# Scores over full 32-row tiles with zero rows, and PV with 32 weight columns

## The chip, the cores and the metric

The kernel runs on one core of a Trainium2 chip. The metric is the device time of one execution in microseconds (us). Before the change it is 1242.52 us, the median of three runs (1239.01 to 1251.18).

## The reference, cut to what matters

A layer norm of x (2048 rows of 512) feeds two branches, and both are added to x. Branch A is attention with 32 heads of 16 dimensions, branch B a gated feed-forward block with 1792 hidden columns.

```python
xn = _layernorm(x)
qkv = (xn @ wqkv)                                  # 2048 x 1536, 32 heads of 16
scores = jnp.einsum("bhqd,bhkd->bhqk", q, k) * (Dh ** -0.5)
p = _softmax(scores, axis=-1)
o = jnp.einsum("bhqk,bhkd->bhqd", p, v)
A = o @ wo
B = (_silu(xn @ w1) * (xn @ w3)) @ w2
return x + A + B
```

## The kernel before

Two programs are planned in Python and emitted, `_plan_fast` and `_plan_max`; the second is only entered when a flag says that the first was out of its numeric range, and it does not run here. All lines named below are of the fast one.

**How it is tiled.** Queries are cut into 4 chunks of 512, heads into 8 groups of 4. A unit is one chunk with one group, 32 units in all. In a unit the keys come in 16 tiles of 128. K and Q lie transposed in SBUF, in `KT` and `QT`: the four heads of a group stand on partitions 0, 32, 64 and 96, each with 16 rows of data and a 17th row of constants (1.0 in `QT`, 127 times 128 in `KT`). Partitions 17 to 31 of each 32 are never written and never read. The constants come from `crow`, four rows in the scratch tile `yb`, by two DMAs (L1095 and L1097).

**Scores** (`score`, L1509): one call issues two matmuls, of two heads, on two 32-row tiles of the array, with 17 rows of weights (`KT`, 128 keys) and 17 rows of moving data (`QT`, 512 queries), into two PSUM banks.

**Exponentials.** A pair of banks goes one of two ways. `try_a` gives it to ScalarE, one ACTIVATE of 128x1024 (L1543). `try_d` gives it to VectorE, which builds exp from integer operations (L1587, L1610, L1604, L1615, L1621) in three parts, and so makes three times as many PV matmuls. L1610 writes the scratch tile `mb`.

**PV** (`try_pv`, L1670): four matmuls side by side, one per head and per 32-column tile of the array. The weights are `Vaug[:, kt, head, :]`, 128 rows by 17 columns (16 of V and a column of ones, which gives the sum of the softmax), the moving data 128x512 probabilities. Results gather in PSUM bank 7, 17 of each 32 partitions; the other partitions of the bank hold zeros from the start. At the end of a unit L1687 copies the bank to `U`, four sums per query are turned into reciprocals by way of small DMAs, and L1723 multiplies `U` by `R`, whose unused partitions are zero.

**Dense matmuls** (`col_groups`, L1204): all projections, the feed-forward block and the output, always four matmuls side by side with 128 rows and 32 columns each.

**The order** is fixed at build time. A planner (`_Sched`) plays the engines' time with assumed costs, for TensorE 0.23 us per group of four, and writes one instruction list per engine. On TensorE it tries ScalarE scores first, then VectorE scores, PV and dense work. Work for the other engines waits in lists filled by `post` and emptied by `pump`, by priority. All DMAs are issued from the SyncE queue in the planned order: the loads of x and wqkv, the constants, then for every K and Q tile the moves from a staging tile `stg` to `KT` and `QT` (L1279), the late loads of the feed-forward weights and wo (L1186 to L1198), and later the small DMAs at the end of each unit.

Of the kernel before, what the change touches and what calls it, by code (L numbers as in the profile page):

```python
# [140 lines left out]
class _Sched(_Prog):  # L141
# [28 lines left out]

    def post(self, eng, emit, ready=0.0, prio=1, cond=None):

        self.seq += 1
        self.pend[eng].append((prio, self.seq, ready, cond, emit))

# [802 lines left out]
def _plan_fast(nc, ps, flag, A_x, A_wqkv, A_wo, B_w1, B_w3, B_w2, out):  # L978
    S, D = A_x.shape[1], A_x.shape[2]
    H = D // 16  # L980
# [30 lines left out]
    with ctx:  # L1011
# [4 lines left out]
        yb = sb("yb", [128, 2, 1024], I16)  # L1016
        mb = sb("mb", [128, 2, 1024], I16)
        crow = yb[0:4, 0, :].bitcast(BF16).rearrange("p (k n) -> p k n", n=512)
        xn_sb = sb("xn_sb", [128, 4, D], BF16)
# [54 lines left out]
        def c_misc(e):  # L1074
            e.memset(crow[:, 0, :], 1.0)
            e.memset(crow[:, 1, :], YB)
            e.memset(ones_t[:, :], 1.0)
            return e.memset(mhalf[:, :], -0.5)
# [5 lines left out]
        for gi in range(1, 4):  # L1084
            P.dma(lambda e, gi=gi: e.dma_start(x_sb[:, 4 * gi:4 * gi + 4, :], x_v[:, 4 * gi:4 * gi + 4, :]),
                  writes=[("x", t) for t in range(4 * gi, 4 * gi + 4)], kb=512)
            if gi == 1:
                P.dma(lambda e: e.dma_start(wv, wqkv_v[:, :, 2 * D:3 * D]), writes=[("wv",)], kb=512)

        P.op("dve", lambda e: e.memset(bank(7), 0.0), writes=[("ps", 7)], dur=0.6)  # L1090
        P.op("pool", c_misc, writes=[("ones_t",), ("mhalf",), ("crow",)], dur=0.8)
        P.op("pool", lambda e: e.affine_select(ident[:, :], ones_t[:, :], [[1, 128]], ALU.is_equal, 0.0,
# [5 lines left out]
                                    crow[:, 1, :].unsqueeze(1).broadcast_to([4, NG * NQC, 512])),  # L1098
              reads=[("crow",)], writes=[("KTc",)], kb=128)

        def fill(eng_dst, val):
# [390 lines left out]
        def score(b0, name, dur):  # L1492
            r0 = st["pos"]
            u, rr = divmod(r0, RPU)
            kt, j0 = divmod(rr, 4)
            g = u % NG
            if not have(("QTm", u), ("KTm", g, kt // 4)):
                return None
            rd = [("QT", u % 4), ("KT", g, kt // 4), ("QTc",), ("KTc",)]
            mms = []  # L1500
            for i in range(2):
                j = j0 + i
                rd += [("QTm", u, j), ("KTm", g, kt // 4, j)]
                mms.append((b0 + i, KT[32 * j:32 * j + 17, g, kt * 128:(kt + 1) * 128],
                            QT[32 * j:32 * j + 17, u % 4, :], 32 * j))

            def f(e, mms=tuple(mms)):
                for (b, l_, r_, rp) in mms:
                    ins = e.matmul(bank(b), l_, r_, start=True, stop=True, tile_position=(rp, 0))  # L1509
                return ins  # L1510
            o = P.op("pe", f, reads=rd, writes=[("ps", b0), ("ps", b0 + 1)], dur=pe_dur("S", dur), name="%s%d" % (name, r0))
            st["pos"] += 2
            return r0, u, j0, kt, o
# [44 lines left out]
        def try_d():  # L1558
# [24 lines left out]
            def p1():  # L1583
# [25 lines left out]
                def f_m():  # L1609
                    P.op("dve", lambda e: e.tensor_scalar(mb[:, ys, :], yb[:, ys, :], 0x7F, 0x3F00,  # L1610
                                                          ALU.bitwise_and, ALU.bitwise_or),
                         reads=[("yb", ys)], writes=[("mb", ys)], dur=0.35)

# [18 lines left out]

        pv_unit = [0]

        def try_pv():
# [22 lines left out]
            for j in sorted(pick):  # L1658
# [4 lines left out]
                stop = st["pos"] >= (u + 1) * RPU and npv[u][j] == NT + 2 * ndj[u][j]  # L1663
                mms.append((j, Vaug[:, tk[1], 4 * g + j, :], tk[2], start, stop))
                rd += [("V", tk[1]), tk[3]]
                rels.append(tk[4])

            def f(e, mms=tuple(mms)):
                for (j, v_, p_, s0, s1) in mms:
                    ins = e.matmul(bank(PV)[32 * j:32 * j + 17, :], v_, p_, start=s0, stop=s1, tile_position=(0, 32 * j))  # L1670
                return ins
# [244 lines left out]
```

## Time and profile before

| | |
|---|---|
| time, median of 3 runs | 1242.52 us (1239.01 to 1251.18) |
| time of the profiled execution | 1237.0 us |
| its span, first to last instruction | 1235.1 us |
| instructions | 21867 |
| mean granted TensorE clock in the span | 0.595 of full speed |
| HBM read, written | 22.81 MB, 2.10 MB |

A page of the profile gives, for one execution, the busy time of each engine: PE is TensorE's matmuls, PEld its weight loads (they overlap the matmuls), DVE is VectorE, ACT ScalarE, POOL GpSimd, SPq the queue from which SyncE issues DMAs. PEclk is the TensorE clock that was granted: 0.50 is 1.2 GHz and 1.00 is 2.4 GHz; a value between them is a stretch with some of each. Matmuls are pipelined, and a busy PE is not one at its peak.

### The profile page before, as it was taken

The numbers are of one execution on the slowest core, as the hardware profiler recorded it, in microseconds if no ns is written. First come the engines' busy times: TensorE is split into PE (matmuls) and PEld (weight loads), VectorE is DVE, ScalarE is ACT, GpSimd is POOL, SyncE is SP. The second block draws the span as 40 slices with busy tenths as digits, with TensorE's granted clock in tenths as the row PEclk, the third lists the DMA queues.
The fourth block names the chain that finished last, engine by engine and source line by source line (L and its number), as shares of the span: only waits on it lengthen the run. The fifth ranks groups of instructions, "written<-read, shape, count | busy, mean of one in ns | idle before, by whom it ended". The sixth has DMA issues, their size and how long they took to land.

```text
span 1235.1 us, 21867 instructions
## 1 busy us (share of the span) xinstructions
PE 1155.8 (94%) x9033; PEld 233.0 (19%) x9033; DVE 829.9 (67%) x1434; ACT 843.2 (68%) x874; POOL 53.5 (4%) x72
## 2 busy tenths in 40 slices
PE   4799999999999999999999999998999999989656
PEld 2222111111111221111111111122211111121123
DVE  5368776677766997766777655689876766657322
ACT  4578777677776997777777666689877776647210
POOL 3000000000000000000000000010000000010000
PEclk9666555555555995555555555579655555575588
DMA  4402122220211131122222110032222210032220
GB/s 133 102 19 33 18 31 23 24 39 12 32 16 12 21 25 27 22 23 27 31 23 23 5 19 10 13 32 28 24 34 23 27 19 9 15 36 27 32 51 30
DMA packets 90837, 35.49 MB, mean 29 GB/s; under 512 B 74456, under 2 KB 88680, under 8 KB 90728
## 3 DMA queue, kind: packets, MB, share of 16 engines
q1 hardware_dynamic: 90728, 34.00, 19.8%
q8 instruction: 73, 1.20, 0.4%
q14 instruction: 36, 0.29, 0.1%
HBM read 22.81 MB, written 2.10 MB: 20 GB/s over the span
## 4 chain that ended last, share of the span: by engine, by line
PE 84%; DVE 8%; DMA 4%; SPq 1%; issue 1%; ACT 1%; POOL 0%; DVEq 0%; POOLq 0%
PE ps L1509 29%; PE ps L1204 29%; PE ps L1670 26%; DVE f_yb L1587 3%; DMA f_w<-in_B_w_dram 2%; DMA f_KT<-f_stg 1%; DVE f_xd L1621 1%; DVE f_mb L1610 1%; DVE f_xd L1604 1%; DMA f_wkv<-in_A_wqkv_dram 1%; DVE f_xd L1615 1%; ACT f_PT L1543 1%; SPq L1279 0%; PE ps L1233 0%; DVE f_hT L1356 0%
## 5 line engine op out<-in xcount | busy, mean ns | idle before, releaser
L1543 ACT ACTIVATE f_PT<-ps 128x1024 bf16<-128x1024 f32 x798 | 798.8, 1027 | 298.8 <-PE ps L1509 258.7
L1509 PE MATMUL ps<-f_QT,f_KT 17*128 17x512 bf16 x2048 | 452.9, 563 | 17.8 <-DMA f_KT<-f_stg 7.4
L1587 DVE TENSOR_SCALAR f_yb<-ps 128x1024 int16<-128x1024 f32 x226 | 276.1, 1222 | 135.6 <-PE ps L1509 127.4
L1670 PE MATMUL ps<-f_PT,f_Vaug 128*17 128x512 bf16 x1596 | 331.7, 562 | 7.3 <-DVE f_xd L1604 5.3
L1670 PE MATMUL ps<-f_xd,f_Vaug 128*17 128x512 bf16 x1356 | 303.9, 570 | 2.9 <-DVE f_xd L1621 2.2
L1204 PE MATMUL ps<-f_xnT,f_w 128*32 128x512 bf16 x1792 | 230.7, 576 | 26.2 <-DMA f_w<-in_B_w_dram 23.7
L1509 PEld LDWEIGHTS ps<-f_QT,f_KT 17*128 17x128 bf16 x2048 | 84.7, 98 | 546.3 <-issue 341.4
L1621 DVE TENSOR_TENSOR f_xd<-f_yb,f_mb 128x1024 bf16<-128x1024 bf16 x226 | 152.3, 683 | 0.0
L1610 DVE TENSOR_SCALAR f_mb<-f_yb 128x1024 int16<-128x1024 int16 x226 | 101.1, 447 | 5.4
L1604 DVE TENSOR_SCALAR f_xd<-f_yb 128x1024 int16<-128x1024 int16 x226 | 100.4, 444 | 0.0
L1204 PE MATMUL ps<-f_w,f_hT 128*32 128x512 bf16 x896 | 97.8, 509 | 2.3 <-DVE f_hT L1356 1.3
L1615 DVE TENSOR_SCALAR f_xd<-f_yb 128x1024 int16<-128x1024 int16 x226 | 96.8, 428 | 0.1
L1356 DVE SCALAR_TENSOR_TENSOR f_hT<-f_t,ps 128x512 bf16<-128x512 bf16 x56 | 38.4, 686 | 74.1 <-PE ps L1204 73.8
L1723 POOL TENSOR_TENSOR f_onorm<-f_U,f_R 128x512 bf16<-128x512 f32 x31 | 41.6, 1342 | 1054.5 <-DMA f_R<-f_Rrow 560.6
L1670 PEld LDWEIGHTS ps<-f_PT,f_Vaug 128*17 128x17 bf16 x1596 | 54.3, 93 | 137.3 <-issue 101.2
L1204 PEld LDWEIGHTS ps<-f_xnT,f_w 128*32 128x32 bf16 x1792 | 47.8, 110 | 113.3 <-issue 76.7
L1670 PEld LDWEIGHTS ps<-f_xd,f_Vaug 128*17 128x17 bf16 x1356 | 49.7, 95 | 88.5 <-issue 53.1
L1342 ACT ACTIVATE f_th<-ps 128x512 f32<-128x512 f32 x56 | 33.6, 599 | 47.9 <-PE ps L1204 47.9
L1346 DVE SCALAR_TENSOR_TENSOR f_t<-f_th,ps 128x512 bf16<-128x512 f32 x56 | 38.2, 683 | 29.2 <-ACT f_th L1342 29.2
L1204 PE MATMUL ps<-f_wo,f_onorm 128*32 128x512 bf16 x512 | 53.0, 494 | 0.1
L1687 DVE COPY f_U<-ps 128x512 f32<-128x512 f32 x32 | 22.0, 689 | 33.4 <-PE ps L1670 28.4
L1204 PE MATMUL ps<-f_xnT,f_wq 128*32 128x512 bf16 x256 | 34.6, 575 | 0.3 <-DVE f_hT L1356 0.3
(48 smaller groups left out, 232.6 us busy)
## 6 DMA issues: line engine op xcount, KB each, us to landing
f_w<-in_B_w_dram SPq DMA_DIRECT2D x112, 128.0 KB, 2.5
f_R<-f_Rrow SPq DMA_DIRECT2D x128, 32.0 KB, 4.0
f_KT<-f_stg SPq DMA_DIRECT2D x128, 16.0 KB, 1.8
f_QT<-f_stg SPq DMA_DIRECT2D x128, 16.0 KB, 1.8
f_xr<-in_A_x_dram SPq DMA_DIRECT2D x16, 128.0 KB
out_dram<-f_xn_sb SPq DMA_DIRECT2D x16, 128.0 KB, 1.7
f_w<-in_B_w_dram SPq DMA_DIRECT2D x1, 1792.0 KB
f_xd<-in_A_x_dram SPq DMA_DIRECT2D x3, 512.0 KB
```

Source lines behind the costliest of these rows:

```text
L1204: ins = e.matmul(bank(bk)[32 * i:32 * i + 32, 0:ncols], make_lhsT(i), rhs_ap, start=start, stop=stop, tile_position=(0, 32 * i))
L1346: q2 = P.op("dve", lambda e: e.scalar_tensor_tensor(t1[:, ss, :], th[:, ss, :], 1.0, bank(bk), ALU.add, ALU.mult), reads=[("th", ss), ("ps ...
L1356: q = P.op("dve", lambda e: e.scalar_tensor_tensor(hT[:, fc, :], t1[:, ss, :], 0.5, bank(bk), ALU.mult, ALU.mult), reads=[("t1", ss), ("ps ...
L1509: ins = e.matmul(bank(b), l_, r_, start=True, stop=True, tile_position=(rp, 0))
L1543: q = P.op("act", lambda e: e.activation(PT[:, s_, :], ps[:, b0 * 512:(b0 + 2) * 512], ACTF.Exp, scale=ASC, bias=A_BIAS), reads=[("ps", b0 ...
L1587: q = P.op("dve", lambda e: e.tensor_scalar(yb[:, ys, :], ps[:, 4 * 512:6 * 512], 0.0, 32767.0, ALU.max, ALU.min), reads=[("ps", 4), ("ps" ...
L1604: q_ = P.op("dve", lambda e: e.tensor_scalar(dsl[:, s_, 0, :], yb[:, ys, :], 0x7F80, None, ALU.bitwise_and), reads=[("yb", ys)], writes=[( ...
L1610: P.op("dve", lambda e: e.tensor_scalar(mb[:, ys, :], yb[:, ys, :], 0x7F, 0x3F00, ALU.bitwise_and, ALU.bitwise_or), reads=[("yb", ys)], wr ...
L1615: q_ = P.op("dve", lambda e: e.tensor_scalar(dsl[:, s_, 1, :], yb[:, ys, :], -352.0, 0.0, ALU.add, ALU.max), reads=[("yb", ys)], writes=[( ...
L1621: q_ = P.op("dve", lambda e: e.tensor_tensor(dsl[:, s_, 2, :].bitcast(BF16), yb[:, ys, :].bitcast(BF16), mb[:, ys, :].bitcast(BF16), ALU.m ...
L1670: ins = e.matmul(bank(PV)[32 * j:32 * j + 17, :], v_, p_, start=s0, stop=s1, tile_position=(0, 32 * j))
L1723: q = P.op(eng, lambda e: e.tensor_tensor(onorm[:, u % NON, :], U[:, us, :], R[:, :], ALU.mult), reads=[("U", us)] + [("R", j_) for j_ in ...
```

## The change

Three things are edited.

- `KT` and `QT` get zeros on partitions 17 to 31 of every 32. The zeros come from `zrow`, 15 rows of the scratch tile `mb`, set by one more GpSimd memset and copied by 20 DMAs: four for `QT`, four for groups 0 and 1 of `KT` right after them, and twelve for the other six groups, posted to SyncE's list with the planner's time 14.0 us. The scores wait for them (keys `QTz` and `KTz`), and the first three writes of `mb` at L1610 wait until they have been read.
- The two matmuls of a score then take 32 rows in place of 17, zeros in the added ones.
- PV takes 32 weight columns of `Vaug` in place of 17, from the same start, so that the 15 added ones are the first columns of the next head. The last head keeps 17. What the added columns give lands on the partitions that nobody reads unscaled; `R` is zero there.

`post` gets a duration and a function `backlog` is added; neither is called with it here.

```diff
--- before.py
+++ after.py
@@ -168,10 +168,13 @@
         op = _Prog.dma(self, fn, reads, writes, name, eng)
         return self._time(op, op.deps, 0.06, 1.9 + kb / 200.0)
 
-    def post(self, eng, emit, ready=0.0, prio=1, cond=None):
+    def post(self, eng, emit, ready=0.0, prio=1, cond=None, dur=0.6):
 
         self.seq += 1
-        self.pend[eng].append((prio, self.seq, ready, cond, emit))
+        self.pend[eng].append((prio, self.seq, ready, cond, emit, dur))
+
+    def backlog(self, eng):
+        return max(0.0, self.free[eng] - self.t) + sum(it[5] for it in self.pend[eng] if it[2] <= self.t + 0.3)
 
     def pump(self, eng):
         best = None
@@ -1015,6 +1018,7 @@
         xr = sb("xr", [128, 2, D], BF16)
         yb = sb("yb", [128, 2, 1024], I16)
         mb = sb("mb", [128, 2, 1024], I16)
+        zrow = mb[0:15, 0, 0:512].bitcast(BF16)
         crow = yb[0:4, 0, :].bitcast(BF16).rearrange("p (k n) -> p k n", n=512)
         xn_sb = sb("xn_sb", [128, 4, D], BF16)
         stats = sb("stats", [128, NT, 6], FP32)
@@ -1074,6 +1078,7 @@
         def c_misc(e):
             e.memset(crow[:, 0, :], 1.0)
             e.memset(crow[:, 1, :], YB)
+            e.memset(zrow[:, :], 0.0)
             e.memset(ones_t[:, :], 1.0)
             return e.memset(mhalf[:, :], -0.5)
 
@@ -1088,7 +1093,7 @@
                 P.dma(lambda e: e.dma_start(wv, wqkv_v[:, :, 2 * D:3 * D]), writes=[("wv",)], kb=512)
 
         P.op("dve", lambda e: e.memset(bank(7), 0.0), writes=[("ps", 7)], dur=0.6)
-        P.op("pool", c_misc, writes=[("ones_t",), ("mhalf",), ("crow",)], dur=0.8)
+        P.op("pool", c_misc, writes=[("ones_t",), ("mhalf",), ("crow",), ("zrow",)], dur=0.8)
         P.op("pool", lambda e: e.affine_select(ident[:, :], ones_t[:, :], [[1, 128]], ALU.is_equal, 0.0,
                                                base=0, channel_multiplier=-1),
              reads=[("ones_t",)], writes=[("ident",)], dur=0.4)
@@ -1097,6 +1102,19 @@
         P.dma(lambda e: e.dma_start(KT[16:128:32, :, :].rearrange("p g (a n) -> p (g a) n", n=512),
                                     crow[:, 1, :].unsqueeze(1).broadcast_to([4, NG * NQC, 512])),
               reads=[("crow",)], writes=[("KTc",)], kb=128)
+
+        def zeros(g0, g1):
+            for j in range(4):
+                P.dma(lambda e, j=j: e.dma_start(
+                    KT[32 * j + 17:32 * j + 32, g0:g1, :].rearrange("p g (a n) -> p (g a) n", n=512),
+                    zrow[:, :].unsqueeze(1).broadcast_to([15, (g1 - g0) * NQC, 512])),
+                    reads=[("zrow",)], writes=[("KTz", g) for g in range(g0, g1)], kb=60 * (g1 - g0))
+        for j in range(4):
+            P.dma(lambda e, j=j: e.dma_start(QT[32 * j + 17:32 * j + 32, :, :],
+                                             zrow[:, :].unsqueeze(1).broadcast_to([15, 4, 512])),
+                  reads=[("zrow",)], writes=[("QTz",)], kb=60)
+        zeros(0, 2)
+        P.post("sp", lambda: [zeros(g, g + 2) for g in range(2, NG, 2)], ready=14.0, prio=2)
 
         def fill(eng_dst, val):
             return lambda e: e.activation(eng_dst, mhalf[:, 0:1].to_broadcast((128, eng_dst.free_size())), ACTF.Copy,
@@ -1500,9 +1518,9 @@
             mms = []
             for i in range(2):
                 j = j0 + i
-                rd += [("QTm", u, j), ("KTm", g, kt // 4, j)]
-                mms.append((b0 + i, KT[32 * j:32 * j + 17, g, kt * 128:(kt + 1) * 128],
-                            QT[32 * j:32 * j + 17, u % 4, :], 32 * j))
+                rd += [("QTm", u, j), ("KTm", g, kt // 4, j), ("QTz",), ("KTz", g)]
+                mms.append((b0 + i, KT[32 * j:32 * j + 32, g, kt * 128:(kt + 1) * 128],
+                            QT[32 * j:32 * j + 32, u % 4, :], 32 * j))
 
             def f(e, mms=tuple(mms)):
                 for (b, l_, r_, rp) in mms:
@@ -1609,7 +1627,7 @@
                 def f_m():
                     P.op("dve", lambda e: e.tensor_scalar(mb[:, ys, :], yb[:, ys, :], 0x7F, 0x3F00,
                                                           ALU.bitwise_and, ALU.bitwise_or),
-                         reads=[("yb", ys)], writes=[("mb", ys)], dur=0.35)
+                         reads=[("yb", ys)], writes=[("mb", ys)] + ([("zrow",)] if nd < ND else []), dur=0.35)
 
                 def f_g():
                     q_ = P.op("dve", lambda e: e.tensor_scalar(dsl[:, s_, 1, :], yb[:, ys, :], -352.0, 0.0,
@@ -1631,6 +1649,12 @@
             return True
 
         pv_unit = [0]
+        Vf = Vaug[:, :, :, :].rearrange("p t h d -> p t (h d)")
+
+        def v_w(kt, h):
+
+            return Vf[:, kt, 17 * h:17 * h + (32 if h < H - 1 else 17)]
+
 
         def try_pv():
             u = pv_unit[0]
@@ -1661,13 +1685,13 @@
                 start = npv[u][j] == 0
                 npv[u][j] += 1
                 stop = st["pos"] >= (u + 1) * RPU and npv[u][j] == NT + 2 * ndj[u][j]
-                mms.append((j, Vaug[:, tk[1], 4 * g + j, :], tk[2], start, stop))
+                mms.append((j, v_w(tk[1], 4 * g + j), tk[2], start, stop))
                 rd += [("V", tk[1]), tk[3]]
                 rels.append(tk[4])
 
             def f(e, mms=tuple(mms)):
                 for (j, v_, p_, s0, s1) in mms:
-                    ins = e.matmul(bank(PV)[32 * j:32 * j + 17, :], v_, p_, start=s0, stop=s1, tile_position=(0, 32 * j))
+                    ins = e.matmul(bank(PV)[32 * j:32 * j + v_.shape[-1], :], v_, p_, start=s0, stop=s1, tile_position=(0, 32 * j))
                 return ins
             o = P.op("pe", f, reads=rd, writes=[("ps", PV)], dur=pe_dur("C", 0.23), name="pv%d" % u)
             for r_ in rels:
```

## Rows read from the trace of the kernel before

**Rows 1.** Page, parts 1, 2, 4: busy us, granted clock by slices, chain

```profile
PE 1155.8 (94%) x9033; PEld 233.0 (19%) x9033; DVE 829.9 (67%) x1434; ACT 843.2 (68%) x874; POOL 53.5 (4%) x72
...
PEclk9666555555555995555555555579655555575588
...
PE 84%; DVE 8%; DMA 4%; SPq 1%; issue 1%; ACT 1%; POOL 0%; DVEq 0%; POOLq 0%
```

**Rows 2.** Windows: stretch, us, busy us (count) of each engine, PEclk, DMA share, GB/s

```profile
77.30:111.40 34.10, 34.10 (x238) 6.06 (x230) 26.58 (x45) 25.69 (x27) 1.40 (x1) 0.50 0.22 30
...
121.70:401.60 279.90, 278.46 (x1922) 48.49 (x1920) 195.84 (x333) 200.73 (x205) 10.56 (x8) 0.50 0.19 23
401.60:466.40 64.80, 60.21 (x692) 15.86 (x684) 62.04 (x108) 61.57 (x66) 4.19 (x3) 1.00 0.25 28
466.40:818.00 351.60, 350.76 (x2408) 59.52 (x2404) 242.70 (x418) 253.30 (x256) 11.71 (x9) 0.50 0.17 19
818.00:876.00 58.00, 51.62 (x548) 14.22 (x546) 56.03 (x97) 55.14 (x62) 4.74 (x4) 1.00 0.34 38
876.00:1084.20 208.20, 207.75 (x1438) 36.10 (x1442) 139.10 (x240) 145.91 (x149) 3.81 (x3) 0.50 0.14 19
...
1098.00:1150.00 52.00, 50.14 (x342) 8.82 (x346) 39.01 (x67) 36.82 (x39) 3.91 (x3) 0.50 0.24 29
```

**Rows 3.** Windows of L1543, the ScalarE exponentials

```profile
121.70:401.60 279.90, 194.46 (x193) 0.50 0.19 23
401.60:466.40 64.80, 61.08 (x65) 1.00 0.25 28
466.40:818.00 351.60, 246.76 (x243) 0.50 0.17 19
818.00:876.00 58.00, 53.47 (x57) 1.00 0.34 38
```

**Rows 4.** Windows of L1587, the first step of the VectorE exponentials

```profile
121.70:401.60 279.90, 67.16 (x55) 0.50 0.19 23
401.60:466.40 64.80, 24.43 (x20) 1.00 0.25 28
466.40:818.00 351.60, 88.03 (x72) 0.50 0.17 19
818.00:876.00 58.00, 19.53 (x16) 1.00 0.34 38
```

**Rows 5.** Windows of L1509, the scores: PE, PEld, PEclk, DMA share, GB/s

```profile
814.70:818.00 3.30, 0.27 (x4) 0.10 (x2) 0.50 0.49 55
...
108.00:111.40 3.40, 1.12 (x8) 0.21 (x6) 0.50 0.30 68
...
230.90:234.30 3.40, 1.18 (x6) 0.17 (x6) 0.50 0.08 20
```

**Rows 6.** Windows of L1670, PV, in the first stretch of rows 5

```profile
814.70:818.00 3.30, 3.15 (x28) 0.82 (x28) 0.50 0.49 55
```

**Rows 7.** Windows, all engines, the last 3.4 us before two falls of the clock

```profile
463.00:466.40 3.40, 2.17 (x28) 0.52 (x25) 3.26 (x5) 3.35 (x4) 1.27 (x1) 1.00 0.51 123
872.60:876.00 3.40, 2.36 (x22) 0.69 (x22) 3.29 (x7) 2.27 (x3) 0.00 (x0) 1.00 0.17 38
```

**Rows 8.** Groups by line: xcount | busy us, mean ns | idle before

```profile
L1670 PEld LDWEIGHTS ps<-f_PT,f_Vaug 128*17 128x17 bf16 x1596 | 54.3, 93 | 137.3 <-issue 101.2 <-DVE f_yb L1587 9.2 <-DVE f_xd L1604 9.1
...
L1204 PEld LDWEIGHTS ps<-f_xnT,f_w 128*32 128x32 bf16 x1792 | 47.8, 110 | 113.3 <-issue 76.7 <-DMA f_w<-in_B_w_dram 30.0 <-DVE f_hT L1356 1.1
```

**Rows 9.** SyncE's queue and chain of waits at the start: start us, us, what

```profile
8.43 0.56 SPq L1097 DMA_DIRECT2D f_KT<-f_yb  x1
19.20 5.03 SPq L1279 DMA_DIRECT2D f_KT<-f_stg  x8
...
34.13 11.15 DMA f_KT<-f_stg
```

**Rows 10.** Page, part 6: DMA issues, KB each, median us to landing

```profile
f_w<-in_B_w_dram SPq DMA_DIRECT2D x112, 128.0 KB, 2.5
```

## The prediction

> **What bounds the kernel now.** I read the page's first two parts first. TensorE is busy 94% of the span, VectorE 67%, ScalarE 68%, and the granted clock stands at 5 in 28 of the 40 slices [rows 1]; in the chain that ended last TensorE has 84% [rows 1]. So TensorE is the bound, at half its clock. Next the windows, cut where the clock changes [rows 2]. There are two kinds of stretch. At 0.50 TensorE is busy throughout (278.46 of 279.90 us, 350.76 of 351.60) while ScalarE and VectorE stand at 70%. At 1.00 TensorE has gaps (60.21 of 64.80) and ScalarE and VectorE are both at 95% (61.57 and 62.04 of 64.80): there they are the bound. The order of instructions is the same fixed list in both; only the clock differs.
>
> What a stretch gets done is counted in score pairs, of which every pair ends in one L1543 or one L1587. At half clock 193 + 55 and 243 + 72 pairs, 563 in 631.5 us, or 1.122 us each; at full clock 65 + 20 and 57 + 16, 158 in 122.8 us, or 0.777 us each [rows 3, 4]. Full clock is worth 1 - 0.777 / 1.122 = 31% of a half-clock stretch, not 50%, since the other two engines then set the pace.
>
> **What moves the clock.** Busy time does not: the two long half-clock stretches are busy over 99%. What the engine did ahead of a change differs. The clock rose at 818.0 us after 3.15 us of PV and 0.27 us of scores [rows 5, 6], and at 111.4 after 3.4 us with 1.12 us of scores; with 1.18 us of scores it did not rise at 234.3 [rows 5]. It fell at 466.4 and 876.0 after TensorE had been busy only 2.17 and 2.36 us of 3.4, waiting for the other two engines [rows 7]. Two things follow. PV with 17 of 32 columns lifted the clock by itself, so idle columns do not count against it. The scores hold it down: a pair of them drives 2 x 17 = 34 of the array's 128 rows, PV and dense work all 128. And the steady mix is near to rising as it is, since two stretches as alike as 1.12 and 1.18 us of scores came out differently.
>
> **Part 1, scores with 32 rows.** The pair then drives 64 of 128 rows. A matmul streams 512 columns as before, so its own time stays. If rows are what counts, a mix that is near to rising with 34 rows rises in most places with 64, and the clock comes up on its own rather than after a chance run of PV or dense work. Half-clock stretches in the middle: 34.1 + 279.9 + 351.6 + 208.2 + 52.0 = 925.8 us [rows 2]. At full clock they save 31%, or 285 us.
>
> The clock will still fall where TensorE waits, as in rows 7. The full-clock stretches of 64.8 and 58.0 us [rows 2] give one fall per 61 us; 925.8 - 285 = 641 us hold 10 or 11. No row shows how soon it comes back with 32 rows. The bounds are 0 and the 34.1 us that the shortest half-clock stretch of rows 2 lasted. I take 11 us, a third, because the mix as a rule rises then. Each costs 31% of that: 10.5 x 11 x 0.31 = 36 us, between 0 and 111.
>
> The Trainium skill speaks against this part. TensorE: Matmul & The Clock Gate, Part 1, says that the gate sets the clock by how busy the PE has been recently, and its section Why this matters for your kernels asks only for continuous busy time; by that the rows of a matmul would not matter, the kernel would already run at full clock, and the change would give the start-up cost only, about 1248 us. This trace does not agree, with 99% busy at 0.50 in rows 2.
>
> **Part 2, PV with 32 columns.** The load of 128x17 weights takes 93 ns, that of 128x32 takes 110 [rows 8]. For 2952 loads (1596 in the row shown, 1356 of the second PV source) that is 2952 x 17 ns = 50 us of loading. It lies beside matmuls: loads take 48.49 of 279.90 us and dense groups already load 32 columns [rows 2, 8]. Cost 0; 50 us if none of it were covered. Gain 0, as 17 columns lifted the clock in rows 6; a gain on top would only make the first part surer.
>
> **Part 3, the zeros.** One memset on GpSimd, busy 53.5 us in the whole span [rows 1], and 20 DMAs on SyncE's queue. A move of its kind occupies the queue 5.03 / 8 = 0.63 us [rows 9], so 20 are 12.6 us. The queue is free from 8.99 to 19.20 us [rows 9]; the eight that the first scores need, 5.0 us, fit in it, and stand ahead of the K and Q moves. The other twelve, 7.6 us, have 5.2 us of it if they come next, and otherwise stand ahead of the late loads and of the second K moves, whose landing TensorE already awaits for 11.15 us [rows 9]. So between 2.4 and 7.6 us are late on the queue. The copies also move 2.2 MB in pieces of some 120 KB; the nearest row is a 128 KB load that lands in 2.5 us [rows 10], 0 if all of it falls in the free time, up to 6 us if it pushes the late loads. I take 6 us on the path, between 0 and 14. The wait at L1610 costs nothing as long as the copies land before VectorE's first exponentials, and otherwise no more than the lateness already counted. What stands behind a late K move on SyncE's queue is the next K move, and for those wait scores and then ScalarE; later in the kernel nothing is added to the queue.
>
> **Sum** against the profiled execution's own 1237.0 us (span 1235.1 and 1.9 around it): - 285 + 36 + 0 + 6 gives 994. The median of the runs is 5.5 us above this execution, or 0.4%, but at a kernel a fifth shorter I carry 4: 998. Its own range: without any fall and start-up cost, 1237 - 285 = 952, and less if the full-clock rate is a little better than 0.777, so 940. With the longest returns and all start-up costs, 1237 - 285 + 111 + 14 + 5.5 = 1083; with PV loads half uncovered 1108.
>
> **Rivals.**
>
> *The clock stays.* If the chip counts occupied time in another form, or a 32-row tile as a whole whether 17 or 32 of its rows are used, or doesn't count rows of zeros, nothing rises. For it: the two stretches with 1.12 and 1.18 us of scores are so alike that something finer than the share of scores decides. Against it: PV alone lifted the clock. Time: 1242.5 + 6 = 1248, no change. It also is the case in which the change doesn't do what it says. Chance 0.19.
>
> *Half of it.* The clock rises, but ScalarE and VectorE pull it down again at full clock as in rows 7, and it comes back late. With returns of 140 us, half of the 279.9 of rows 2, a round is 61 us at 0.777 and 140 us at 1.122 us a pair, 78.5 + 124.8 = 203.3 pairs in 201 us, or 0.989 us each. The 825 pairs of 925.8 us (at 1.122) then take 816 us and save 110: 1237 - 110 + 6 + 5.5 = 1139, and with shorter or longer returns 1108 to 1225. For it: no row shows a return. Against it: the mix is near to rising already. Chance 0.12.
>
> *Slower.* The mechanism is SyncE's queue at the start: if all 20 copies come ahead of the first K moves, these go out at 8.99 + 12.6 = 21.6 in place of 19.2 us, and the late loads and second K moves follow 7.6 us and 6 us of data later. The clock staying at half, all of 14 us is on the path: 1242.5 + 14 = 1257, 1.1% slower. It decides from 12.4 us on the path and only where the clock doesn't rise. Chance 0.07.
>
> **How the numbers follow.** My forecast, 940 to 1108, has chance 0.62; half of it 0.12; the clock stays 0.19; slower 0.07. Faster by over 1% (12.4 us, about what a measurement of this kernel can tell from no change) has 0.62 + 0.12 = 0.74, within 1% 0.19, slower 0.07. The predicted time is that of the likeliest, 998. For 8 in 10 the range takes in the second case and part of the third, up to its centre: 945 to 1248. The likeliest case's own range is 940 to 1108.
>
> **What would show it.** Right: the clock's row at 9 in most slices after the start, the mean of the scores' matmuls down from that of before, ScalarE and VectorE near 90% between 100 us and the end of the exponentials, full-clock stretches that end only behind a wait for those two engines. The added rows show as 32-row scores and 128x32 PV loads at about 110 ns, beside matmuls. The copies show as 20 rows in SyncE's queue with the late loads a few us later. Wrong: a row of fives with TensorE at 99% means that the chip doesn't count rows as I read it; a clock that rises and pairs at over 0.8 us each mean a new bound; a start over 14 us late means that the copies' cost was undersized. If PV loads show up as idle time of TensorE, part 2 was not free.

## The result, and the profile after

The changed kernel takes 1034.24 us, the median of four executions (1032.24 to 1035.08), beside 1240.76 us for the kernel before (median of four). The ratio is 0.8321, with a 95% interval of 0.8270 to 0.8372. The profiled execution took 1034.6 us with a span of 1032.8; its mean granted clock is 0.902, before 0.595. The forecast was 998 us, so the direction and the mechanism held and 36 us are missing.

The page of the kernel after, parts 1, 2, 4, 5 and 6 (busy us, granted clock by slices, chain, groups by line, DMA issues with KB and us to landing):

```profile
PE 846.4 (82%) x9041; PEld 234.8 (23%) x9041; DVE 827.4 (80%) x1444; ACT 796.0 (77%) x872; POOL 53.9 (5%) x73
...
PEclk9685979798899999979999899988989999989679
...
DVE 48%; PE 28%; DMA 9%; ACT 5%; issue 4%; SPq 4%; POOL 0%; DVEq 0%; POOLq 0%
...
L1527 PE MATMUL ps<-f_QT,f_KT 32*128 32x512 bf16 x2048 | 345.3, 405 | 87.1 <-DVE f_yb L1605 25.7
...
L1694 PEld LDWEIGHTS ps<-f_PT,f_Vaug 128*32 128x32 bf16 (+1 forms) x1592 | 56.4, 94 | 97.6 <-issue 58.6
...
f_KT<-f_mb SPq DMA_DIRECT2D x16, 120.0 KB, 3.3
```

The row of fives in [rows 1] has become a row with 8 or 9 in 33 of its 40 places. TensorE's share of the chain fell from 84% to 28%, and VectorE has 48% of it: the bound has moved. The lines have moved as well: L1509 is L1527 now, L1543 is L1561, L1587 is L1605, L1670 is L1694, L1279 is L1297.

Windows of the kernel after, as in [rows 2]: stretch, us, busy us (count) of TensorE, its weight loads, VectorE, ScalarE, GpSimd, then clock, DMA share, GB/s. Three long stretches at full clock, and the whole middle, from where the window counts 29 pairs to the end of the last exponential.

```profile
277.50:441.50 164.00, 150.19 (x1658) 41.38 (x1654) 158.34 (x275) 158.12 (x172) 8.89 (x7) 1.00 0.24 27
...
455.00:523.50 68.50, 58.62 (x648) 16.43 (x648) 65.16 (x112) 65.19 (x73) 3.83 (x3) 1.00 0.31 38
...
574.50:687.50 113.00, 104.67 (x1166) 28.39 (x1162) 108.75 (x188) 107.89 (x117) 5.33 (x4) 1.00 0.22 23
...
112.50:951.50 839.00, 745.42 (x7782) 197.46 (x7782) 758.61 (x1311) 750.69 (x818) 41.38 (x31) 0.93 0.24 29
```

The same three stretches for L1561 alone (ScalarE's exponentials), then for L1605 alone (VectorE's), as in [rows 3, 4]:

```profile
277.50:441.50 164.00, 155.55 (x165) 1.00 0.24 27
455.00:523.50 68.50, 62.58 (x66) 1.00 0.31 38
574.50:687.50 113.00, 107.19 (x115) 1.00 0.22 23
```

L1605:

```profile
277.50:441.50 164.00, 59.91 (x49) 1.00 0.24 27
455.00:523.50 68.50, 22.01 (x18) 1.00 0.31 38
574.50:687.50 113.00, 41.56 (x34) 1.00 0.22 23
```

That is 346 + 101 = 447 pairs in 345.5 us, or 0.773 us each, where 0.777 was forecast. VectorE and ScalarE are at 95 to 97% there: full clock is worth no more because of them.

**The balance.** Cut the span in three. The start, until 29 pairs are counted, ended at 77.3 us before and ends at 112.5 now: +35.2. The middle, to the end of the last exponential, was 1073.4 us (to 1150.7) and is 839.0 (to 951.5): -234.4. The tail was 84.4 and is 81.3: -3.1. Together -202.3, which is 1032.8 - 1235.1.

**Where the start went.** SyncE's queue in the kernel after (start us, us, what), and below it the two rows of its waits on its own copies (us in total, times, longest us):

```profile
9.53 15.70 SPq L1113 DMA_DIRECT2D f_QT<-f_mb  x4
25.27 10.89 SPq L1108 DMA_DIRECT2D f_KT<-f_mb  x4
36.21 5.03 SPq L1297 DMA_DIRECT2D f_KT<-f_stg  x8
41.28 5.02 SPq L1297 DMA_DIRECT2D f_QT<-f_stg  x8
46.34 33.98 SPq L1108 DMA_DIRECT2D f_KT<-f_mb  x12
80.42 15.11 SPq L1297 DMA_DIRECT2D f_KT<-f_stg  x24
```

The waits:

```profile
SPq L1108 <- DMA f_KT<-f_mb: 30.4, 12, 3.0
SPq L1113 <- DMA f_QT<-f_mb: 11.9, 3, 7.1
```

The 20 zero copies hold the queue for 15.70 + 10.89 + 33.98 = 60.6 us, and for 42.3 us of it the queue waits for the copy before to land. The cause stands in the diff: four copies write four different strips of partitions but all name the same key, `("QTz",)` or `("KTz", g)`, so the program makes each wait for the one before. The K moves start at 36.21 us where they started at 19.20 [rows 9], and the first scores follow. TensorE's timeline, the first score of the kernel before and then of the kernel after (in brackets the idle time ahead of it):

```profile
26.96 0.61 PE L1509 MATMUL ps<-f_QT,f_KT 17*128 17x512 bf16 x2 [2.79 <-DMA f_QT<-f_stg]
```

And after:

```profile
43.98 0.61 PE L1527 MATMUL ps<-f_QT,f_KT 32*128 32x512 bf16 x2 [18.12 <-DMA f_QT<-f_stg]
```

The Trainium skill, DMA: Bandwidth & Descriptors, section Anatomy of one DMA (written for the GpSimd path), says that most of a DMA's fixed cost is the wait for its completion, and that a wait on a semaphore is served by the sequencer that issues, ahead of the dispatch. The rows on SyncE's waits agree with the second: it is SyncE's queue that waits, 30.4 us in 12 waits, each behind a copy that takes 3.3 us to land. How a landing divides into moving and completing, no run here shows.

### The profile page after: what moved, and what is told of

It is laid out like the page before. It is cut to its first block, busy times and chain, and to the rows that moved or that the text cites. A ratio compares the mean times of both kernels' runs of the same rounds, so it can differ in the third digit from the quotient of the medians.

```text
span 1032.8 us, 21915 instructions
## 1 busy us (share of the span) xinstructions
PE 846.4 (82%) x9041; PEld 234.8 (23%) x9041; DVE 827.4 (80%) x1444; ACT 796.0 (77%) x872; POOL 53.9 (5%) x73
## 3 DMA queue, kind: packets, MB, share of 16 engines
q1 hardware_dynamic: 93188, 36.21, 25.4%
## 4 chain that ended last, share of the span: by engine, by line
DVE 48%; PE 28%; DMA 9%; ACT 5%; issue 4%; SPq 4%; POOL 0%; DVEq 0%; POOLq 0%
DVE f_yb L1605 18%; PE ps L1222 12%; PE ps L1527 8%; PE ps L1694 8%; DVE f_xd L1639 7%; DVE f_mb L1628 6%; DVE f_xd L1622 5%; DVE f_xd L1633 5%; ACT f_PT L1561 4%; DMA f_KT<-f_mb 4%; SPq L1297 3%; DMA f_w<-in_B_w_dram 2%; DVE f_hT L1374 2%; DVE f_t L1364 2%; DMA f_QT<-f_mb 1%
## 5 line engine op out<-in xcount | busy, mean ns | idle before, releaser
L1561 ACT ACTIVATE f_PT<-ps 128x1024 bf16<-128x1024 f32 x796 | 757.7, 1051 | 144.1 <-PE ps L1527 131.9
L1527 PE MATMUL ps<-f_QT,f_KT 32*128 32x512 bf16 x2048 | 345.3, 405 | 87.1 <-DVE f_yb L1605 25.7
L1605 DVE TENSOR_SCALAR f_yb<-ps 128x1024 int16<-128x1024 f32 x228 | 278.3, 1221 | 59.1 <-PE ps L1527 46.2
L1694 PE MATMUL ps<-f_PT,f_Vaug 128*32 128x512 bf16 (+1 forms) x1592 | 239.4, 408 | 12.8 <-DVE f_xd L1622 8.4
L1694 PE MATMUL ps<-f_xd,f_Vaug 128*32 128x512 bf16 (+1 forms) x1368 | 218.4, 407 | 14.1 <-DVE f_xd L1639 8.2
L1222 PE MATMUL ps<-f_xnT,f_w 128*32 128x512 bf16 x1792 | 172.3, 443 | 49.2 <-DMA f_w<-in_B_w_dram 34.3
L1527 PEld LDWEIGHTS ps<-f_QT,f_KT 32*128 32x128 bf16 x2048 | 83.6, 91 | 410.9 <-ACT f_PT L1561 208.9
L1694 PEld LDWEIGHTS ps<-f_PT,f_Vaug 128*32 128x32 bf16 (+1 forms) x1592 | 56.4, 94 | 97.6 <-issue 58.6
L1694 PEld LDWEIGHTS ps<-f_xd,f_Vaug 128*32 128x32 bf16 x1368 | 51.9, 95 | 83.9 <-issue 33.6
L1222 PE MATMUL ps<-f_w,f_hT 128*32 128x512 bf16 x896 | 69.9, 382 | 0.2 <-DVE f_stg L1289 0.2
L1222 PE MATMUL ps<-f_wo,f_onorm 128*32 128x512 bf16 x512 | 42.3, 382 | 0.2 <-DVE f_wkv L1414 0.2
L1240 DVE CAST f_Vaug<-ps 128x512 bf16<-128x512 f32 x16 | 11.0, 689 | 28.4 <-PE ps L1222 28.4
```

Of the source, the lines that this page charges most:

```text
L1222: ins = e.matmul(bank(bk)[32 * i:32 * i + 32, 0:ncols], make_lhsT(i), rhs_ap, start=start, stop=stop, tile_position=(0, 32 * i))
L1561: q = P.op("act", lambda e: e.activation(PT[:, s_, :], ps[:, b0 * 512:(b0 + 2) * 512], ACTF.Exp, scale=ASC, bias=A_BIAS), reads=[("ps", b0 ...
L1605: q = P.op("dve", lambda e: e.tensor_scalar(yb[:, ys, :], ps[:, 4 * 512:6 * 512], 0.0, 32767.0, ALU.max, ALU.min), reads=[("ps", 4), ("ps" ...
L1694: ins = e.matmul(bank(PV)[32 * j:32 * j + v_.shape[-1], :], v_, p_, start=s0, stop=s1, tile_position=(0, 32 * j))
```

## The experiments

Six questions, by their runs. Lines are those of the kernel that is edited. Times are medians; a ratio is to the kernel before as it was measured beside the run, where its medians were 1248.8, 1241.4 and 1244.2 us. "Half clock in the middle" is read from windows of 0.5 us between the 29th pair and the last exponential, in the one profiled execution of each run.

**1. Do the added rows do it, or something else in the change?** Zeros copied, PV on 32 columns, but scores back on 17 rows. The instruction lists of all engines are those of the changed kernel.

```diff
-                mms.append((b0 + i, KT[32 * j:32 * j + 32, g, kt * 128:(kt + 1) * 128],
-                            QT[32 * j:32 * j + 32, u % 4, :], 32 * j))
+                mms.append((b0 + i, KT[32 * j:32 * j + 17, g, kt * 128:(kt + 1) * 128],
+                            QT[32 * j:32 * j + 17, u % 4, :], 32 * j))
```

> The changed kernel with the scores back on 17 rows: the zeros are still copied and PV keeps its 32 columns. Theory rows: the clock is that of the kernel before (near 0.60), and the time is that of before plus the late start, 1241 + 25 to 40 = 1266 to 1281. Rival columns: the clock lies between, the time below 1200.

Measured: 1334.16 us (1332.13 to 1334.78), ratio 1.0698 (1.0642 to 1.0753). The page's row of the granted clock:

```profile
PEclk9755555555555555555555555555555555585569
```

Its middle, in the columns of the long windows above:

```profile
115.00:1248.00 1133.00, 1126.24 (x7790) 202.57 (x7786) 764.52 (x1310) 806.36 (x817) 41.91 (x31) 0.51 0.18 21
```

With one difference, rows of zeros in the two operands of the scores, the same lists take 1334 or 1034 us. So the rows do it, and zeros in them count. In this order the rows are worth 300 us; without them the change costs 85, by 1334.16 and the 1248.8 of the kernel before beside it. That cost is more than expected, and the next run looks at it.

The same with PV on 17 columns as well, so that only the copies and the order of the changed kernel are left:

```diff
-            return Vf[:, kt, 17 * h:17 * h + (32 if h < H - 1 else 17)]
+            return Vf[:, kt, 17 * h:17 * h + 17]
```

> The changed kernel with its zero copies and its order, but scores on 17 rows and PV on 17 weight columns: the change's costs without its rows. In the same order, scores on 17 rows with PV on 32 columns took 1334 us at a mean clock of 0.54. Theory A (PV columns play no part): 1325 to 1340 us as well. Theory B (with 17-row scores the 32 PV columns cost stretches of full clock, as the PV-only kernel's 1277 against 1241 us in the order of before suggests): 1290 to 1315 us, mean clock 0.56 to 0.60.

Measured: 1328.15 us, ratio 1.0677 (1.0632 to 1.0722), an interval that overlaps that of the run above: here the columns change nothing that can be told. Without its rows the change costs 84 us by the medians and 92 by the two profiled executions (1329.1 and 1237.0). Of the 92, 38 are the late start: this run has 29 pairs at 115.7 us, the kernel before at 77.3. The rest is lost full clock. The kernel before had 1073 - 926 = 147 us of it in its middle, this run has 24; what 123 us get done at 0.777 us a pair takes 178 us at 1.122, 55 more. Together that is 93. Why the clock rises less often in this order, no run shows.

**2. How much do the rows do?** Zeros and scores cut to 20, 24 and 28 rows, the lists unchanged but for the size of the zeros. Here 24:

```diff
-        zrow = mb[0:15, 0, 0:512].bitcast(BF16)
+        zrow = mb[0:7, 0, 0:512].bitcast(BF16)
...
-                    KT[32 * j + 17:32 * j + 32, g0:g1, :].rearrange("p g (a n) -> p (g a) n", n=512),
+                    KT[32 * j + 17:32 * j + 24, g0:g1, :].rearrange("p g (a n) -> p (g a) n", n=512),
...
-                mms.append((b0 + i, KT[32 * j:32 * j + 32, g, kt * 128:(kt + 1) * 128],
-                            QT[32 * j:32 * j + 32, u % 4, :], 32 * j))
+                mms.append((b0 + i, KT[32 * j:32 * j + 24, g, kt * 128:(kt + 1) * 128],
+                            QT[32 * j:32 * j + 24, u % 4, :], 32 * j))
```

> The changed kernel with zeros and score tiles cut to 20 rows, same order. Measured at 17, 24, 28 and 32 rows: 1334, 1069, 1063 and 1034 us. Theory A (a graded dose): between 1090 and 1290 us, mean clock 0.57 to 0.80. Theory B (a step just past 17 rows): 1060 to 1085 us, clock about 0.82. Theory C (a step between 20 and 24 rows): 1320 to 1340 us.

> The changed kernel with its zeros and its score tiles cut from 32 to 24 rows; the order of every engine's instructions stays the same, and the scores on 17 rows in that order took 1334 us, on 32 rows 1034 us. Theory A (a dose): with about half of the added rows the full-clock time lies between the two, 1080 to 1290 us, mean clock 0.6 to 0.85. Theory B (a full tile is what counts, 32 rows or not): 1320 to 1340 us, mean clock about 0.54. Theory C (any rows past 17 do): 1030 to 1050 us, clock about 0.90.

> The changed kernel with its zeros and its score tiles cut from 32 to 28 rows, same order. Theory A (a dose): 1035 to 1200 us, mean clock 0.7 to 0.9, and faster than the 24-row kernel of the same call. Theory B (only a full tile counts): 1320 to 1340 us. Theory C (any rows past 17 do): 1030 to 1050 us.

| rows of a score | us | half clock in the middle, us | spells of it | mean spell, us |
|---|---|---|---|---|
| 17 | 1334 | 1109 of 1132 | 2 | 554 |
| 20 | 1207 (1150 to 1217) | 798 of 1030 | 7 | 114 |
| 24 | 1069 (1065 to 1078) | 281 of 879 | 14 | 20 |
| 28 | 1063 (1060 to 1068) | 233 of 864 | 18 | 13 |
| 32 | 1034 | 109 of 839 | 15 | 7.3 |

The granted clock by slices, from the pages of the three kernels. 20 rows:

```profile
PEclk9755555555557999555555559955567755585669
```

24 rows:

```profile
PEclk9675755598759999985995899998887959987589
```

28 rows:

```profile
PEclk9575585798788999987997699996899989968679
```

(With 20 rows the four executions lie between 1150.4 us, at a mean clock of 0.713, and 1216.8 us at 0.632. The profile is of the longest, so this row of the table is one end of a spread.) The 1069 us of 24 rows lie between theory A (from 1080) and theory C (up to 1050) and meet neither. As a whole this is a graded dose, neither a step at the full tile nor one just past 17; 24 and 28 rows are not told apart by their times. From 24 rows on the number of falls hardly changes (14, 18, 15); what changes is how long the clock stays down, 20, 13 and 7.3 us in the mean.

**3. Do the PV columns matter?** The changed kernel with PV on 17 columns (the edit shown above alone):

> The changed kernel with PV back at 17 weight columns; scores keep their 32 rows. Theory rows: the clock comes from the scores' rows alone, so the time is that of the changed kernel, 1024 to 1044, clock near 0.90. Rival columns: the added PV columns gave part of the clock; then the mean clock falls below 0.85 and the time is above 1060.

Measured: 1030.08 us, ratio 0.8264 (0.8212 to 0.8316), its interval overlapping that of the changed kernel, 0.8270 to 0.8372. And the kernel before with 32 columns alone:

```diff
-                mms.append((j, Vaug[:, tk[1], 4 * g + j, :], tk[2], start, stop))
+                mms.append((j, v_w(tk[1], 4 * g + j), tk[2], start, stop))
```

> The kernel before with one part of the change alone: the PV products take 32 weight columns, the scores stay at 17 rows, no zeros are filled. Theory A (the clock answers to the rows that the scores drive): the time of the kernel before, 1233 to 1250 us, mean granted clock 0.59 to 0.60, weight loads of the PV pairs at 110 ns or less and hidden. Theory B (the active columns count too, as the change says in its name): the mean clock rises above 0.65 and the time falls below 1200 us.

Measured: 1277.24 us. Its six executions lie in two groups of three, 1264.7 to 1267.2 and 1287.3 to 1289.4, and the ratio of the lower group is 1.0198 (1.0154 to 1.0241). No theory expected a loss: the instruction lists are those of the kernel before. The loss goes with the clock, which is 0.566 to 0.570 in the lower group, against 0.587 to 0.599 in six of the eight executions of the kernel before beside it. Why 2% are lost here, and nothing between 1328 and 1334 us in the pair of question 1, stays open.

**4. Is it the shared key that makes the start late?** Each copy gets a key of its own, and the scores wait for the four they need:

```diff
-                    reads=[("zrow",)], writes=[("KTz", g) for g in range(g0, g1)], kb=60 * (g1 - g0))
+                    reads=[("zrow",)], writes=[("KTz", g, j) for g in range(g0, g1)], kb=60 * (g1 - g0))
...
-                  reads=[("zrow",)], writes=[("QTz",)], kb=60)
+                  reads=[("zrow",)], writes=[("QTz", j)], kb=60)
...
-                rd += [("QTm", u, j), ("KTm", g, kt // 4, j), ("QTz",), ("KTz", g)]
+                rd += [("QTm", u, j), ("KTm", g, kt // 4, j), ("QTz", j), ("KTz", g, j)]
```

> Each of the 20 zero copies gets a dependency key of its own, so that none waits for the landing of the one ahead of it; all else is as in the changed kernel. Theory A, the start is late because the copies go out one by one (3.3 us each from issue to landing, where SyncE's queue needs 0.63 us to issue one): the copies take about 13 us of the queue in place of 61, the first scores come near 27 to 30 us in place of 44, and the time falls by 25 to 35 us, to about 1000 to 1009. Rival B, the start is late because of the bytes (2.2 MB): the copies still end late and the time stays within 10 us of 1034.

Measured: 1028.22 us (1018.62 to 1039.04), ratio 0.8202 (0.8128 to 0.8275): 6 us gained where 25 to 35 were expected, and the interval touches that of the changed kernel. The time is the one that rival B gave, but not for its reason: the waits of the queue on its copies are gone, and the last copy has left the queue at 38.5 us, in place of 80.3. What went wrong is the order. The planner counts an issue as 0.06 us, and now that no copy waits for another it puts all sixteen K copies ahead of the first K moves, as SyncE's queue shows:

```profile
9.34 8.48 SPq L1113 DMA_DIRECT2D f_QT<-f_mb  x4
17.86 20.67 SPq L1108 DMA_DIRECT2D f_KT<-f_mb  x16
38.65 2.72 SPq L1297 DMA_DIRECT2D f_KT<-f_stg  x2
```

The 29th pair comes at 95 us (112.5 before the edit), and the middle takes 848.8 us where it took 839.0: with other keys the planner makes another order of the whole kernel. So 17.5 us are gained at the start, and 9.8 are lost again in the middle and 2.2 in the tail.

The other way to have no copies: nine GpSimd memsets over whole tiles, in elements of 4 bytes.

```diff
+        def ktz(g):
+            P.op("pool", lambda e: e.memset(KT[:, g, :].bitcast(FP32), 0.0), writes=[("KTz", g)], dur=1.05)
...
+        P.op("pool", lambda e: e.memset(QT[:, :, :].rearrange("p a n -> p (a n)").bitcast(FP32), 0.0), writes=[("QTz",)], dur=1.05)
```

> The zeros are written by GpSimd memsets over whole rows of QT and of each group of KT (nine of 128x1024 in 4-byte elements, about 1 us each by the 0.51 us of a 512-column memset) ahead of the constants and the moves; no zero copies on SyncE's queue at all. Theory A: the start is as in the kernel before, so 30 to 38 us come back: 996 to 1005, and no slower than the run with a key for each copy. Rival: the memsets hold up GpSimd's layer norm steps and the start loses 5 to 10 us of that again.

Measured: 1033.81 us, ratio 0.8272 (0.8216 to 0.8328), no gain at all. The start is back (29 pairs at 77 us), so the rival's loss at the start is not there either, but the middle takes 872.5 us, 33 more than in the changed kernel. Its window:

```profile
77.00:949.50 872.50, 762.86 (x7810) 198.86 (x7812) 767.79 (x1323) 752.83 (x817) 40.62 (x31) 0.91 0.23 28
```

Half clock takes 160 us of it in 23 spells, against 109 us in 15. At 31% that is 16 of the 33 us; the other 17 are not assigned. Both kernels changed the start and the order at once, so they could not settle the question. What they do settle, with question 2, is that bytes are not the cause: with 20 rows a K copy has 24 KB in place of 120, and the 20 copies, which still wait for each other, hold the queue for 13.8 + 8.7 + 26.9 = 49.4 us in place of 60.6.

**5. The same edit in the same order.** Own keys again, but the copies are planned at the times that the chain of waits gave them, so that the lists of all engines are those of the changed kernel and only the waits between copies are gone:

```diff
+        zlast = [None]
+
+        def zplan(f):
+            if zlast[0] is not None:
+                P.free["sp"] = max(P.free["sp"], zlast[0].end + _LAT)
+            zlast[0] = f()
...
-                P.dma(lambda e, j=j: e.dma_start(
+                zplan(lambda j=j: P.dma(lambda e, j=j: e.dma_start(
...
-                    reads=[("zrow",)], writes=[("KTz", g) for g in range(g0, g1)], kb=60 * (g1 - g0))
+                    reads=[("zrow",)], writes=[("KTz", g, j) for g in range(g0, g1)], kb=60 * (g1 - g0)))
```

> The changed kernel with a key of its own for each zero copy, so that no copy waits for another, but with the planned order of the changed kernel kept (line numbers apart), which the kernel with own keys and a new order did not keep. Theory A (the start's gain of some 20 us was eaten by the other order's extra spells of half clock): the first scores come 10 to 20 us earlier, the half-clock time of the middle stays near the changed kernel's 109 us, and the time is 1010 to 1022 us. Theory B (the start's gain is lost to the middle in any order, since VectorE and ScalarE set its pace): 1028 to 1038 us.

Measured: 1005.27 us (995.84 to 1014.50), ratio 0.8027 (0.7994 to 0.8061), below even the 1010 to 1022 expected. SyncE's queue:

```profile
9.45 8.65 SPq L1120 DMA_DIRECT2D f_QT<-f_mb  x4
18.15 4.37 SPq L1115 DMA_DIRECT2D f_KT<-f_mb  x4
22.57 6.47 SPq L1305 DMA_DIRECT2D f_KT<-f_stg  x8
...
34.14 14.96 SPq L1115 DMA_DIRECT2D f_KT<-f_mb  x12
```

The middle:

```profile
85.00:917.60 832.60, 740.24 (x7786) 197.52 (x7782) 757.01 (x1312) 751.76 (x819) 39.99 (x31) 0.95 0.24 29
```

The 20 copies hold the queue for 28.0 us in place of 60.6. The first K moves start at 22.57 us, 13.6 earlier, and the 29th pair comes at 85 us, 27.5 earlier. The middle takes 832.6 us, 6.4 less (half clock takes 88 us of it in place of 109, which at 31% is 7), and the tail 3.2 more, so the gain stays. This shows that the waits between the copies cost the changed kernel some 28 us at the start, and, beside the kernel with own keys in a new order, that the order decides whether such a gain is kept.

**6. PV columns once more, in the faster kernel.** With 17 columns, and once more with 32 beside it:

> The kernel with own keys in the changed kernel's order, with PV back on 17 weight columns. Theory A (the PV columns give nothing at 32-row scores): within 1% of the run with 32 columns in the same call, about 1000 to 1012 us. Theory B (they help to hold the clock): 1015 to 1040 us, with more time at half clock. Theory C (they cost clock, as with 17-row scores): 975 to 995 us.

> The kernel with own keys in the changed kernel's order once more, as the partner of the run with 17 PV columns: 1000 to 1012 us, as measured before (1005 us).

Measured: 1004.46 us with 17 columns, ratio 0.8049 (0.8002 to 0.8096), and 997.28 us with 32, ratio 0.8021 (0.7987 to 0.8054), the latter a little under the 1000 expected. The intervals overlap: with 32-row scores the columns are worth nothing that can be measured. With either number of columns, the kernel of question 5 is the fastest one here.

## Why the prediction came out as it did

**What bounds the kernel, and what moves the clock: right.** That 99% busy at half clock leaves only the kind of work as a cause was the step that carried the forecast, and question 1 confirms it with everything else held: 1334 against 1034 us. The rival in which rows don't count, or zeros don't, is out. So is the rule weighed there, of the Trainium skill, TensorE: Matmul & The Clock Gate, Part 1, in its plain reading that only busy time counts: the runs here don't agree, as the one with 17 rows has TensorE busy 1126 of 1133 us of its middle at a clock of 0.51, the one with 32 rows 745 of 839 at 0.93. One premise of the step does not hold: that the mix of the kernel before is near to rising as it is. In the changed order 17 rows stay at half clock for 1059 us in one piece, and 20 rows for 798 of 1030 us; the clock is up in most places only from 24 rows on.

**The full-clock rate: right.** 0.773 us a pair in three long stretches, forecast 0.777 from [rows 3, 4].

**The falls: right in sum by luck, with both factors off.** Forecast were 10 or 11 falls of 11 us, 36 us at 31%. The middle has 15 spells of half clock of 7.3 us each, 109 us, or 34 us at 31%: more falls than forecast, and shorter ones, and the two errors cancel. Eleven of the 15 begin where the prediction said, behind a wait for the other two engines: in the last 3.4 us TensorE was busy for 1.97 to 2.57 us and VectorE for 3.10 to 3.37. Windows of the last 3.4 us before two of them, as in [rows 7], and of the half-clock spell behind the second:

```profile
438.10:441.50 3.40, 2.42 (x24) 0.64 (x22) 3.29 (x7) 3.40 (x5) 0.00 (x0) 1.00 0.00 0
520.10:523.50 3.40, 2.33 (x26) 0.73 (x26) 3.10 (x7) 3.32 (x5) 0.00 (x0) 1.00 0.02 5
...
523.50:527.00 3.50, 3.50 (x24) 0.61 (x18) 1.66 (x2) 2.37 (x3) 0.00 (x0) 0.52 0.00 0
```

TensorE works 2.42 and 2.33 us of 3.4 beside two engines that are full; then it is slow and full itself, and the clock comes back. With 17 rows such a spell lasted 279.9 and 351.6 us [rows 2]. The other four spells begin in another way, after TensorE had done next to nothing while neither of the other two was full:

```profile
127.60:131.00 3.40, 0.00 (x0) 0.00 (x0) 0.00 (x0) 1.23 (x2) 0.00 (x0) 0.99 0.08 20
185.60:189.00 3.40, 0.28 (x2) 0.00 (x0) 0.82 (x2) 1.39 (x2) 0.00 (x0) 1.00 0.12 26
243.60:247.00 3.40, 0.00 (x0) 0.00 (x0) 0.07 (x1) 0.00 (x0) 0.00 (x0) 1.00 0.12 25
909.10:912.50 3.40, 0.27 (x2) 0.00 (x0) 1.15 (x3) 1.66 (x2) 0.74 (x1) 1.00 0.45 51
```

The next paragraph says what they waited for.

**The middle: 14.6 us short.** It gave 234.4 us of the forecast 285 - 36 = 249. The shortfall lies at its beginning: from 112.5 to 277.5 us 137 + 38 = 175 pairs are done in 165 us, 0.943 each. There 41 us are at half clock and 124 at full, in which the two rates, 1.122 and 0.777, would give 196 pairs; 21 pairs at 0.777 are 16 us. (By the same sum the rest of the middle is 20 pairs short, but so was the middle of the kernel before, by 18, and these two about cancel.) The rows of that stretch of the kernel after, for L1561:

```profile
112.50:277.50 165.00, 130.35 (x137) 0.88 0.24 31
```

L1605:

```profile
112.50:277.50 165.00, 46.20 (x38) 0.88 0.24 31
```

VectorE's wait (us in total, times, longest us):

```profile
DVE f_Rc L1729 <- DMA f_Lc<-f_U: 18.3, 3, 7.7
```

VectorE waits 18.3 us in that stretch for the four sums at the end of a unit; the kernel before had 4.7 us of that wait between 77.3 and 300 us. While VectorE waits, the other two engines run dry. These three waits, and one more of 4.1 us that ends at 911.35 us, are the four standstills above, and the clock falls in or right behind each. In each of the three the small DMA that brings the sums stands behind 16 or 24 K moves on SyncE's queue. The first:

```profile
113.69 16.71 SPq L1297 DMA_DIRECT2D f_KT<-f_stg  x24
130.50 0.64 SPq L1717 DMA_DIRECT2D f_Lc<-f_U  x1
```

The wait comes with full clock and not with the order. The run of question 1 with 17 rows has the same lists, and there it is short (115 to 350 us):

```profile
DVE f_Rc L1729 <- DMA f_Lc<-f_U: 4.3, 3, 1.9
```

Nor does it come from the waits between the zero copies: the kernel of question 5, which has none of those, still waits 16.7 us for these sums between 85 and 250 us. What the prediction lacked is thus that at full clock the engines come to the end of a unit before SyncE's queue has worked off its K moves; it held only that nothing is added to the queue later in the kernel. That fits the 16 us in size, but no run took this wait away, so its price is argued, not shown. The full-clock rate of the prediction came from two late stretches, in which the kernel before had none of this wait.

**PV columns: right**, at 0, wherever the scores have 32 rows. The loads that were to take 110 ns take 94, at mostly full clock, where 17 columns take 88 (question 3), and stay beside matmuls: all weight loads together rise from 229.4 to 234.8 us. The loss of 2% with 17-row scores (question 3) was not foreseen.

**The zero copies: wrong, by 29 us.** The term said 6 us, between 0 and 14; the start is 35.2 us late, which is the prediction's own sign that the cost was undersized. Two steps failed. The first is that of the price in the queue: 0.63 us a copy was taken from K moves of 16 KB [rows 9]; where no copy waits, 20 of them hold the queue for 28.0 us (question 5), 1.4 each. The second weighs more. The prediction took the copies as issued one behind the other without a wait, although the diff gives four copies one key, and so put the wait of one copy for the landing of another at nothing. Landing one by one is 15 waits, 42.3 us by the rows of SyncE's waits, and the K moves are late by the part of it ahead of them. Without those waits the 29th pair is 7.7 us later than before (85 against 77.3), inside the 0 to 14 of the term. So what the added work costs on the path was about right, in spite of the price of a copy, and the wait that the keys add was missing.

**Sum.** 994 + 29 (start) + 15 (middle) - 3 (tail) = 1035, the profiled execution's 1034.6.

**The rivals that leave the clock** were mis-sized, for the same reason and one more. They were put at 1248 and 1257 us; the run that has all of the change but the rows and the columns took 1328, by the late start and by fewer stretches of full clock in its order. Had the clock not answered, the time would have been far outside the range.

## What to carry to other kernels

Where TensorE is busy all the time at half clock, look at how many rows of the array its matmuls drive; padding a contraction with zeros up to the tile costs no matmul time and took the clock here from 0.595 to 0.902, 17% of the time, after which the other engines are the bound. When a change adds several DMAs, look at which dependency keys they share before pricing them, since each wait on a landing (42.3 us in 15 waits, 2.8 each, here) holds up the whole queue behind it. And compare variants of a planned kernel in one order: two edits that saved 18 and 35 us at the start lost two thirds or all of it in the order that the planner made of them, and the first of them in the old order kept its gain.

## What the runs showed of the hardware

- Rows that hold only zeros, in weights and in moving data, act on the granted clock: 1334 us with 17 rows, 1034 with 32 in the same order. The rows of the weights and those of the moving data were always changed together.
- The number of driven rows acts on how long the clock stays at 1.2 GHz after a fall more than on the number of falls: 114, 20, 13 and 7.3 us a spell with 20, 24, 28 and 32 rows, in 7, 14, 18 and 15 spells, which is a fall in every 33, 43, 35 and 49 us of full clock. Each figure is from one execution.
- PV weight loads of 128x32 took 94 and 95 ns (their two sources) in the changed kernel, at mostly full clock, where 128x17 took 88 (question 3). At mostly half clock they took 105 and 109 ns in the kernel with 32 PV columns alone, where 128x17 had taken 93 [rows 8] and 95.
- A copy of zeros over 15 partitions holds SyncE's queue for 1.1 to 2.2 us in the mean without any wait on another: 8.65 us for the first four, of 60 KB, 4.37 us for the next four and 14.96 us for the last twelve, of 120 KB (question 5). A K move of 16 KB took 0.63 us [rows 9].
